# Stores of the paired-head tiles in 8 KB DMA packets, loads kept at 32 KB

## The chip, the cores and the metric

The kernel runs on one core of one Trainium2 chip, with the chip's other cores idle. The time is device time of one execution, in microseconds; executions of one kernel mostly agree within 0.3%. The core has 16 DMA engines, which move all loads and stores. In the profile's lines PE is the matrix engine (TensorE) and PEld its weight loads, ACT is ScalarE, DVE VectorE, POOL GpSimd and SP SyncE; a q after a name (SPq) is that engine's instruction queue. A transfer has landed when all 16 DMA engines have reported their part of it done, through a counter called a semaphore.

## The reference

It is the forward and backward pass of attention with one query per head. `k` and `v` (2 x 32 heads x 8192 x 128, bfloat16) are read, and gradients `dk`, `dv` of the same size are written, so 268 MB come in and 268 MB go out.

```python
scores = jnp.einsum("bhqd,bhkd->bhqk", q, k) * scale      # Sq = 1
p = softmax(scores)
out = jnp.einsum("bhqk,bhkd->bhqd", p, v)
_out, vjp = jax.vjp(fwd, q, k, v)
return (out, *vjp(grad_out))                              # out, dq, dk, dv
```

## The kernel before

Two heads form a pair; the pair's K (or V) is one tile of 128 partitions x 32 KB. Six such tiles are in SBUF, the core's on-chip memory. A tile is loaded, transposed and multiplied, then overwritten in place by its gradient and stored; only when that store has landed may the next load use the buffer. Loads are issued from SyncE (SP), stores from GpSimd (POOL). Whole tiles move in one DMA; each partition's 32 KB is one contiguous run in memory, so one tile is 128 packets of 32 KB, eight for each DMA engine.

```python
load_eng = nc.sync
store_eng = nc.gpsimd

def load(i, w, pieces=(NCH,)):                 # w: 0 is K, 1 is V
    t = kvp.tile([P, NT, D], BF16, tag=f"kv{slot_of(i, w)}", name="kvt")
    ...
    pin(load_eng.dma_start(out=t[:, n0:n1, :], in_=src[:, n0:n1, :]))

def outer(i, w, c, ends):                      # dk or dv in place of k or v
    pin(nc.vector.tensor_tensor(out=h.tile[w][:, n0 : n0 + CH, :]..., op=ALU.mult))
    if c + 1 in ends:
        ...
        pin(store_eng.dma_start(out=dst[:, b0:b1, :], in_=h.tile[w][:, b0:b1, :]))

# ... cut ...
whole = [NCH]
last_v = [NCH // 2, NCH]                       # the last pair is stored in parts
last_k = [NCH // 2, NCH - 2, NCH - 1, NCH]
for g in range(...):                           # 16 steps per pair, three pairs in flight
    if (i := at(O1 + NCH)) is not None and i + 3 < NP: load(i + 3, 0)
    if (i := at(O0 + NCH)) is not None and i + 3 < NP: load(i + 3, 1)
    if x := within(O1): outer(x[0], 1, x[1], last_v if x[0] == NP - 1 else whole)
    if x := within(O0): outer(x[0], 0, x[1], last_k if x[0] == NP - 1 else whole)
    ...                                        # transposes, scores, softmax, sums
```

Of the kernel before, what the change touches and what calls it, by code (L numbers as in the profile page):

```python
# [17 lines left out]
NG = 2  # L18
GH = 2
NTILE = 6  # L20


@with_exitstack
def kernel(
# [28 lines left out]
    store_eng = nc.gpsimd  # L53
    pin = tc.keep_in_program_order
# [25 lines left out]
    def slot_of(i, w):  # L80

        n = 2 * i + w
        return n if n < NTILE else slot_of(i - NTILE // 2, 1 - w)

    def load(i, w, pieces=(NCH,)):
        h = pairs_[i]
        t = kvp.tile([P, NT, D], BF16, tag=f"kv{slot_of(i, w)}", name="kvt")
        h.tile[w] = t
        src = (v_v if w else k_v)[i]
        c = 0  # L90
        for m in pieces:
            n0, n1 = c * CH, (c + m) * CH
            pin(load_eng.dma_start(out=t[:, n0:n1, :], in_=src[:, n0:n1, :]))  # L93
            c += m
# [7 lines left out]
    load(0, 1)  # L102
    for j in range(1, min(NTILE // 2, NP)):
        load(j, 0)
# [18 lines left out]
    for g in groups:  # L123
# [3 lines left out]
            out=par[g : g + CW], in_=rows.rearrange("p b h -> p h b"), axis=AX.X  # L127
# [298 lines left out]
    def outer(i, w, c, ends):  # L426

        h = pairs_[i]
        n0 = c * CH
        shape = [P, CH, D // 2, 2]  # L430
        pin(
            nc.vector.tensor_tensor(  # L432
                out=h.tile[w][:, n0 : n0 + CH, :].rearrange("p n (e t) -> p n e t", t=2),
                in0=h.qb[w][:]
                .rearrange("p (e t) -> p e t", t=2)
                .unsqueeze(1)
                .to_broadcast(shape),
                in1=h.pair[w][:, n0 : n0 + CH, :].unsqueeze(2).to_broadcast(shape),
                op=ALU.mult,
            )  # L440
        )
        if c + 1 in ends:
            at = ends.index(c + 1)
            b0, b1 = (ends[at - 1] if at else 0) * CH, (c + 1) * CH
            dst = (dv_v if w else dk_v)[i]
            pin(store_eng.dma_start(out=dst[:, b0:b1, :], in_=h.tile[w][:, b0:b1, :]))  # L446

    A1 = NCH + 4
    O1 = A1 + 1
# [7 lines left out]
    for g in range(SL * NP + O0 + NCH + 4 - SL):  # L457
# [15 lines left out]
        if x := within(O1):  # L473
            outer(x[0], 1, x[1], last_v if x[0] == NP - 1 else whole)
        if x := within(O0):
            outer(x[0], 0, x[1], last_k if x[0] == NP - 1 else whole)
# [77 lines left out]
```

## Time and profile before

The median was 1309.53 us of 3 runs (1307.43 to 1312.01).

| what | before |
|---|---|
| DMA queues' share of 16 engines' span | loads 49.5%, stores 48.2% |
| busy: PE / ACT / DVE | 88% / 75% / 65% |
| rate over the span, loads and stores alone | 410 GB/s |
| issue to landing, whole tile | load 27.8 us, store 40.2 us |

These are lines of the page of the kernel before: busy time of each engine, DMA busy tenths in 40 slices, and the DMA queues (packets, MB, share of the 16 engines' span).

```profile
PE 1147.5 (88%) x19108; PEld 849.1 (65%) x19108; DVE 850.5 (65%) x1551; ACT 984.3 (75%) x641; POOL 37.4 (3%) x76
...
DMA  9999999999999999999999999999999999999968
...
DMA packets 19933, 539.58 MB, mean 412 GB/s; under 512 B 2480, under 2 KB 2480, under 8 KB 2992
...
q1 hardware_dynamic: 9968, 268.51, 49.5%
q0 software_dynamic: 9792, 268.44, 48.2%
```

The two DMA queues add up to nearly 98%, and only the last two of 40 slices are not at 9: the DMA engines are the bound. PE comes next, but it mostly has work because data are there.

The page's lines of DMA issues (count, KB each, median us from issue to landing), and the line of the GpSimd issues among the groups (busy us, mean ns of one, idle time before):

```profile
out_dram<-kvt POOLq DMA_DIRECT2D x62, 4096.0 KB, 40.2
kvt<-in_v_dram SPq DMA_DIRECT2D x32, 4096.0 KB, 27.8
kvt<-in_k_dram SPq DMA_DIRECT2D x31, 4096.0 KB, 27.9
```

```profile
L446 POOL DMA_DIRECT2D out_dram<-kvt x68 | 36.3, 534 | 1261.7 <-DVE kvt L432 632.9
```

Who waits, from the waits of the SP queue and of all engines (us in total, times, longest):

```profile
SPq L93 <- DMA out_dram<-kvt: 1188.3, 58, 59.9
```

```profile
PE tp L183 <- DMA kvt<-in_k_dram: 76.8, 27, 5.0
...
PE tp L183 <- DMA kvt<-in_v_dram: 50.5, 27, 3.5
```

SP waits 1188 us for stores to land, because a landed store frees the buffer of a load. PE loses 127 us to loads, in pieces of a few us.

The table of stretches (from:to, length, busy us of each engine, then PE's clock, DMA share, GB/s):

```profile
100.00:200.00 100.00, 97.08 (x1713) 72.49 (x1711) 76.64 (x141) 88.02 (x59) 3.19 (x6) 0.98 1.01 430
200.00:400.00 200.00, 178.63 (x2968) 132.21 (x2965) 131.99 (x239) 152.75 (x100) 5.32 (x10) 0.92 1.00 427
400.00:600.00 200.00, 177.03 (x2940) 130.58 (x2938) 130.11 (x238) 150.97 (x100) 5.32 (x10) 0.92 1.00 419
600.00:800.00 200.00, 178.48 (x2933) 131.79 (x2929) 129.54 (x236) 150.99 (x99) 4.78 (x9) 0.91 1.00 413
1250.00:1265.00 15.00, 12.01 (x191) 8.77 (x189) 8.45 (x15) 9.88 (x6) 0.53 (x1) 0.89 0.76 323
1265.00:1270.00 5.00, 5.00 (x85) 3.75 (x85) 2.69 (x5) 4.17 (x4) 0.00 (x0) 0.99 0.17 72
1270.00:1275.00 5.00, 5.00 (x92) 3.61 (x89) 4.51 (x11) 4.84 (x6) 0.53 (x1) 1.00 0.03 10
```

The rate is 430 GB/s early and 413 to 419 after 400 us. Near the end there is a hole: at 1265-1275 us the DMA engines are nearly idle (shares 0.17 and 0.03). The chain of work that ended last, by engine:

```profile
issue 78%; DMA 14%; PE 3%; POOL 2%; DVE 1%; SPq 0%; POOLq 0%; ACT 0%; DVEq 0%; ACTq 0%
```

Below the page lie the packet records (queue, start, duration, size of every DMA packet). Several figures in this document are worked out from them. The undisturbed duration of a packet, called its minimum here, is 1213 ns for 32 KB, 611 for 16 KB, 309 for 8 KB, 159 for 4 KB: most packets take exactly that, and a few take 2 or 3 ns less. "Excess" below is the sum of what packets take above their minimum, divided by 16 engines.

### The profile page before, as it was taken

The page shows a single profiled execution, that of the slowest core. Times are in us where ns is not written, and L with a number is a line of the kernel's source. Part 1 is how long each engine was busy: PE and PEld are TensorE (multiplying, and loading weights), DVE is VectorE, ACT ScalarE, POOL GpSimd, SP SyncE. Part 2 cuts the span into 40 slices and gives each one's busy share as a digit, 9 for nine tenths or more (in the row PEclk, how much of TensorE's full clock was granted, in tenths as well). Part 3 has the DMA queues.
Part 4 walks back from the last instruction along what each step waited for, and adds up shares of the span by engine and source line. Part 5 has one row for each costly group of instructions (what it writes and reads, how often), then busy time and mean ns, then how long its engine had stood idle before and what let it go on. Part 6 is the DMA issues. An engine that isn't in the chain of part 4 may idle for free.

```text
span 1310.5 us, 41375 instructions
## 1 busy us (share of the span) xinstructions
PE 1147.5 (88%) x19108; PEld 849.1 (65%) x19108; DVE 850.5 (65%) x1551; ACT 984.3 (75%) x641; POOL 37.4 (3%) x76
## 2 busy tenths in 40 slices
PE   5999998898988988989889898898998988888894
PEld 4777766676766666666666676666666666666661
DVE  0677875766766767657676675665766757566666
ACT  5999987876877877778777787777876878777770
POOL 0000000000000000000000000000000000000000
PEclk9999998998989989889898898988988989888896
DMA  9999999999999999999999999999999999999968
GB/s 399 429 374 429 427 429 427 429 428 428 427 424 417 429 422 421 413 415 418 414 413 412 411 417 420 413 417 419 403 421 411 421 408 414 425 404 423 414 257 348
DMA packets 19933, 539.58 MB, mean 412 GB/s; under 512 B 2480, under 2 KB 2480, under 8 KB 2992
## 3 DMA queue, kind: packets, MB, share of 16 engines
q1 hardware_dynamic: 9968, 268.51, 49.5%
q0 software_dynamic: 9792, 268.44, 48.2%
q8 instruction: 149, 2.44, 0.7%
q14 instruction: 24, 0.20, 0.0%
HBM read 268.47 MB, written 268.47 MB: 410 GB/s over the span
## 4 chain that ended last, share of the span: by engine, by line
issue 78%; DMA 14%; PE 3%; POOL 2%; DVE 1%; SPq 0%; POOLq 0%; ACT 0%; DVEq 0%; ACTq 0%
DMA kvt<-in_v_dram 11%; DMA out_dram<-kvt 3%; POOL out_dram L446 2%; PE tp L183 1%; DVE kvt L432 1%; PE acc L376 1%; PE dpw L194 1%; POOLq L446 0%; PE sw L194 0%; ACT ev L185 0%; DVE sel L399 0%; SPq L93 0%; SPq L100 0%; PE sw L222 0%; PE acc L413 0%
## 5 line engine op out<-in xcount | busy, mean ns | idle before, releaser
L185 ACT COPY ev<-tp 128x2048 bf16<-128x2048 bf16 x512 | 954.0, 1865 | 293.6 <-PE tp L183 276.1
L183 PE MATMUL tp<-ident_bf,kvt 128*128 128x128 bf16 x8192 | 585.3, 229 | 127.3 <-DMA kvt<-in_k_dram 76.8
L432 DVE TENSOR_TENSOR kvt<-qb,pair 128x2048 bf16<-128x2048 bf16 x512 | 615.3, 1219 | 49.6 <-PE acc L376 46.7
L183 PEld LDWEIGHTS <-kvt 128*128 128x128 bf16 x8192 | 505.1, 103 | 137.2 <-DMA kvt<-in_k_dram 79.1
L194 PEld LDWEIGHTS <-ev 128*128 128x128 bf16 x8192 | 239.9, 96 | 218.0 <-issue 135.4
L376 PE MATMUL acc<-kvt,E_pad 128*64 128x512 bf16 x1024 | 173.1, 421 | 0.0
L376 PE MATMUL acc<-kvt,dS_pad 128*64 128x512 bf16 x1024 | 169.4, 416 | 1.0 <-DVE dS_pad L362 1.0
L194 PE MATMUL sw<-qdT,ev 128*128 128x2 bf16 x4096 | 142.0, 164 | 2.2 <-ACT ev L185 2.2
L194 PE MATMUL dpw<-qdT,ev 128*128 128x2 bf16 x4096 | 142.2, 164 | 1.0 <-ACT ev L185 1.0
L270 DVE CUSTOM_DVE_ANT_0 junk<-E_f,dpw 64x128 bf16<-64x128 f32 x64 | 18.3, 285 | 144.1 <-PE dpw L194 143.7
L207 DVE TENSOR_REDUCE mp<-sw 64x1 f32<-64x128 f32 x64 | 18.5, 289 | 108.5 <-PE sw L194 108.1
L446 POOL DMA_DIRECT2D out_dram<-kvt x68 | 36.3, 534 | 1261.7 <-DVE kvt L432 632.9
L399 DVE SCALAR_TENSOR_TENSOR sel<-acc,diag,sel 128x128 f32<-128x128 f32 x192 | 67.3, 351 | 6.8
L376 PEld LDWEIGHTS <-dS_pad 128*64 128x64 bf16 x1024 | 38.2, 112 | 29.4 <-issue 6.3
L376 PEld LDWEIGHTS <-E_pad 128*64 128x64 bf16 x1024 | 37.7, 112 | 26.8 <-issue 6.5
L262 DVE CAST E_pad<-E_f 64x128 bf16<-64x128 f32 x64 | 15.3, 239 | 48.5 <-ACT E_f L252 48.5
L413 PE MATMUL acc<-par,sel 128*128 128x2 f32 x128 | 22.0, 241 | 8.0 <-DVE sel L399 8.0
L176 DVE CAST qb<-dpw 128x128 bf16<-128x128 f32 x64 | 18.2, 284 | 13.4 <-PE dpw L167 13.4
L413 PEld LDWEIGHTS acc<-par,sel 128*128 128x128 f32 x128 | 19.7, 195 | 9.5 <-DVE sel L399 9.5
L340 DVE TENSOR_SCALAR negdelta<-dpw,rl 128x1 f32<-128x1 f32 x32 | 7.0, 218 | 27.0 <-PE dpw L300 27.0
L252 ACT ACTIVATE E_f<-sw,negm 64x128 f32<-64x128 f32 x64 | 23.2, 362 | 1.6
L352 DVE SCALAR_TENSOR_TENSOR dSu<-dpw,negdelta,E_f 64x128 f32<-64x128 f32 x64 | 22.4, 350 | 2.1
(49 smaller groups left out, 230.1 us busy)
## 6 DMA issues: line engine op xcount, KB each, us to landing
out_dram<-kvt POOLq DMA_DIRECT2D x62, 4096.0 KB, 40.2
kvt<-in_v_dram SPq DMA_DIRECT2D x32, 4096.0 KB, 27.8
kvt<-in_k_dram SPq DMA_DIRECT2D x31, 4096.0 KB, 27.9
out_dram<-kvt POOLq DMA_DIRECT2D x3, 2048.0 KB, 8.7
kvt<-in_k_dram SPq DMA_DIRECT2D x1, 2048.0 KB, 11.5
kvt<-in_k_dram SPq DMA_DIRECT2D x2, 512.0 KB, 4.5
kvt<-in_k_dram SPq DMA_DIRECT2D x1, 1024.0 KB, 6.9
out_dram<-kvt POOLq DMA_DIRECT2D x1, 1024.0 KB, 7.6
```

Of the source, the lines that this page charges most:

```text
L183: pin(nc.tensor.transpose(tp[:, t, :], src[:, c * CH + t, :], ident_bf[:]))
L185: pin(nc.scalar.copy(out=ev[:], in_=tp[:]))
L194: nc.tensor.matmul(dst[:, c * CH + t, :], lhsT=ev[:, t, :], rhs=qdT[:, w, GH * i : GH * (i + 1)], start=True, stop=True,)
L207: pin(nc.vector.reduce_max(out=h.mp[hs], in_=h.s[hs, :, g], axis=AX.X))
L252: nc.scalar.activation(out=h.E_f[hs], in_=h.s[hs, :, g], func=ACT.Exp, bias=h.negm[hs], scale=scale, accum_out=h.ld[hs, g : g + 1],)
L270: nc.vector.tensor_tensor_reduce(out=junk[hs], in0=h.E_f[hs], in1=h.dp[hs, :, g], scale=1.0, scalar=0.0, op0=ALU.mult, op1=ALU.add, accum_ ...
L352: nc.vector.scalar_tensor_tensor(out=dSu[hs], in0=h.dp[hs, :, g], scalar=negdelta[hs], in1=h.E_f[hs], op0=ALU.add, op1=ALU.mult,)
L376: nc.tensor.matmul(h.acc[w][g : g + CW, :], lhsT=wts[:, n0 * GH : n0 * GH + CW], rhs=rows[:, n0 : n0 + QT, :].rearrange("p n d -> p (n d)" ...
L399: nc.vector.scalar_tensor_tensor(out=h.sel[:], in0=block, scalar=diag[:, b : b + 1], in1=h.sel[:], op0=ALU.mult, op1=ALU.add,)
L413: nc.tensor.matmul(h.acc[w][:, 0:GH], lhsT=h.sel[:], rhs=par[:], start=True, stop=True)
L432: nc.vector.tensor_tensor(out=h.tile[w][:, n0 : n0 + CH, :].rearrange("p n (e t) -> p n e t", t=2), in0=h.qb[w][:] .rearrange("p (e t) -> ...
L446: pin(store_eng.dma_start(out=dst[:, b0:b1, :], in_=h.tile[w][:, b0:b1, :]))
```

## The change

The intent: an engine alternates between its load and store queue packet by packet. If a store packet is a quarter of a load packet, loads get four fifths of the bytes while both have work. Loads then land earlier, and compute waits less.

```diff
+RUN_S = 8192
...
-            pin(store_eng.dma_start(out=dst[:, b0:b1, :], in_=h.tile[w][:, b0:b1, :]))
+            pin(
+                store_eng.dma_start(
+                    out=dst[:, b0:b1, :], in_=h.tile[w][:, b0:b1, :], max_dma_last_dim=RUN_S
+                )
+            )
```

No instruction moves. The 62 whole-tile stores get four descriptors per partition, three half tiles get two, the last small ones stay as they were.

## The prediction

> **What bounds it now.** The DMA engines: the page gives the load queue 49.5% and the store queue 48.2% of 16 engines' span, and the slices show DMA at 9 in all but the last two. PE is busy 88%, ACT 75%. In the waits, PE loses only 127 us to loads, in pieces of 3 to 5 us, while SP spends 1188 us waiting for a store to land before it may refill a buffer. The table of stretches moves 430 GB/s at 100-200 us, 427 at 200-400, but 413 to 419 from 400 to 1000 us.
>
> The trace's packet records say why. An undisturbed 32 KB packet takes 1213 ns (8 KB 309): about 8 ns plus 0.0368 ns per byte. On an engine load and store packets alternate, as the Trainium skill says ("DMA: Bandwidth & Descriptors", Queues, rings and completion order: round-robin at packet granularity). Store packets average 1230 ns, load packets 1264: some 25 us per engine over the minimum, nearly all after 400 us. Those slow loads (1.4 to 2.3 us each) come in bursts where the store queue has run dry and loads run alone just after a store; from 100 to 400 us, with a backlog of stores, there are next to none.
>
> **What the change does.** No instruction moves; 65 of 68 stores get 4 or 2 descriptors per partition. Store-queue packets go from 9,792 to about 33,984.
> - Cost: 4 x 309 against 1213 ns, 23 ns per 32 KB, 496 per engine: +11.4 us of engine time, all on the bound resource (an estimate from those packets).
> - Shift: alternation is by packet, so while both queues have work loads get four fifths of the bytes, not half. A load should land 14-17 us after issue instead of 27.8; a store in 45-50 instead of 40.2. In a saturated ring of six tiles this alone gains nothing.
> - Gain 1: stores queue up behind loads, the store queue seldom runs dry, and part of the slow-load bursts goes: 0 to -20 us; I take -11.
> - Gain 2: around 1250-1275 us the engines idle for about 12.6 us (DMA shares 0.76, 0.17, 0.03 in those stretches), since the last load lands late and later stores wait for compute. With loads first, a backlog of stores fills that hole: -5 to -10; I take -7.
> - Possible loss: four times the software-made descriptors on GpSimd. An issue now takes 0.53 us and the first packet came 3.2 us later; backlog hides growth unless it nears the 20 us cadence.
>
> Sum: 1309.5 + 11.4 - 11 - 7 = 1303 us.
>
> **What would show it.** Right: 8 KB store packets at 309-315 ns; load issue-to-landing nearly halved, store landing longer; PE's waits on loads down; mean load packet at 1220-1240 ns; the hole before the last stores gone, so that the chain of waits ends on stores.
> Wrong: loads still average 1264 or more (then 1310-1315); the hole remains; or GpSimd issues lengthen to microseconds.
>
> **What would make it wrong.** One engine already runs its store packets at about 1300 ns; if that excess is per descriptor, not per byte, it would quadruple there and cost over 5%. The tail's 16 and 8 KB stores show no such growth, so I give it a small chance. In the other direction, if slow loads vanish and the hole closes, about 1285 us.
>
> Predicted 1303 us, range 1283 to 1328. Faster by over 2%: 0.14; within 2%: 0.75; slower by over 2%: 0.11.

## The result

With the change the median is 1307.99 us (1306.05 to 1309.61, 4 runs), before 1309.26 us. The ratio is 0.9988, 95% interval 0.9965 to 1.001. A ratio here is the mean time of one kernel's fast runs over that of the other's in the same rounds, so it is not quite the ratio of the medians. A later repeat gave 0.9999 (0.9986 to 1.0012). The time did not move, to within 0.2%.

The same lines of the page, with the change:

```profile
PE 1136.5 (87%) x19108; PEld 844.3 (65%) x19108; DVE 850.3 (65%) x1551; ACT 984.7 (75%) x641; POOL 51.1 (4%) x76
...
DMA  9999999999999999999999999999999999999987
...
DMA packets 44126, 539.58 MB, mean 413 GB/s; under 512 B 2481, under 2 KB 2481, under 8 KB 2993
...
q0 software_dynamic: 33984, 268.44, 49.7%
q1 hardware_dynamic: 9968, 268.51, 48.8%
```

```profile
out_dram<-kvt POOLq DMA_DIRECT2D x62, 4096.0 KB, 49.7
kvt<-in_v_dram SPq DMA_DIRECT2D x32, 4096.0 KB, 18.9
kvt<-in_k_dram SPq DMA_DIRECT2D x31, 4096.0 KB, 18.6
```

```profile
L448 POOL DMA_DIRECT2D out_dram<-kvt x68 | 50.0, 736 | 1240.0 <-DVE sel L394 637.2
```

Loads land in 18.6 to 18.9 us instead of 27.8, and stores in 49.7 instead of 40.2: the order at the engines did change as intended. The load queue's share fell from 49.5% to 48.8%, but the store queue's rose from 48.2% to 49.7%. A GpSimd issue takes 0.74 us instead of 0.53.

```profile
SPq L94 <- DMA out_dram<-kvt: 1196.1, 58, 60.0
```

```profile
PE tp L184 <- DMA kvt<-in_v_dram: 91.7, 26, 6.1
...
PE tp L184 <- DMA kvt<-in_k_dram: 36.0, 22, 5.1
```

The waits did not shrink: PE lost 127 us to loads before and 91.7 + 36.0 = 128 us now, though each load is over 9 us faster. SP still waits 1196 us, since stores land later.

```profile
100.00:200.00 100.00, 98.42 (x1763) 73.81 (x1761) 78.05 (x143) 90.64 (x60) 4.47 (x6) 1.00 1.01 420
200.00:400.00 200.00, 175.49 (x2939) 130.28 (x2936) 131.95 (x238) 152.10 (x100) 7.44 (x10) 0.92 1.01 422
400.00:600.00 200.00, 176.60 (x2927) 131.06 (x2927) 129.50 (x236) 149.92 (x98) 7.44 (x10) 0.91 1.01 420
600.00:800.00 200.00, 179.18 (x2991) 132.65 (x2991) 132.94 (x242) 154.11 (x102) 7.45 (x10) 0.92 1.00 418
1250.00:1265.00 15.00, 12.49 (x197) 9.08 (x196) 7.32 (x15) 10.51 (x10) 0.00 (x0) 0.89 0.87 356
1265.00:1270.00 5.00, 5.00 (x102) 4.06 (x100) 4.89 (x9) 4.83 (x3) 0.74 (x1) 1.00 0.63 256
1270.00:1275.00 5.00, 4.34 (x63) 2.13 (x60) 3.90 (x8) 2.09 (x2) 0.71 (x1) 1.00 1.01 413
```

The early rate fell from 430 to 420 GB/s, the later one rose from 413-419 to 418-420. The hole in the tail is partly filled (shares 0.87, 0.63, 1.01 in place of 0.76, 0.17, 0.03).

```profile
issue 86%; DMA 7%; POOL 3%; DVE 1%; PE 1%; SPq 0%; POOLq 0%; ACT 0%; DVEq 0%; ACTq 0%
```

The DMA part of the chain is 7% now (by line 4% stores and 3% V loads), where it was 14% (11% V loads and 3% stores).

### Where the time went

The packet records allow an account, in us per engine. "Overlap" is time in which more packets are on record than there are engines: a packet starts 3 to 4 ns before its predecessor on the same engine ends. "Idle" is time with fewer than 16 packets in flight, after the first load packet. Each column comes from one profiled run, so differences of 1 to 2 us mean little. The profiled run of the kernel before (1312.01 us) was also the slowest of its four, that of the change (1308.33 us) an average one.

| | before | the change | difference |
|---|---|---|---|
| packets at their minimum duration | 1242.6 | 1254.2 | +11.6 |
| overlap | -4.0 | -8.8 | -4.8 |
| excess of load packets | 26.4 | 16.0 | -10.4 |
| excess of store packets | 9.1 | 16.0 | +6.9 |
| idle engines | 20.0 | 14.6 | -5.4 |
| sum of these rows' differences | | | -2.1 |
| span of the profiled run | 1310.5 | 1306.6 | -3.9 |
| median of all runs | 1309.26 | 1307.99 | -1.3 |

The rows repeat in other profiles. e9, the change once more, differs from before by +11.6, -4.4, -10.1, +6.4 and -4.9 us. e8, whose first 28 pairs run as before, has a load excess of 24.3 and a store excess of 7.5 us; e7, whose first 28 pairs run as in the change, has 16.8 and 15.7.

So the change made loads cheaper and the tail fuller as hoped. The smaller packets and a new excess on the stores took it back. The experiments ask whether this account holds: what a small packet really costs, whether the order of loads and stores is worth anything, where the excess comes from, and how much of it is tail.

### The profile page after: what moved, and what is told of

The parts are those of the page before. It is cut to its first block, busy times and chain, and to the rows that moved or that the text cites. A ratio compares the mean times of both kernels' runs of the same rounds, so it can differ in the third digit from the quotient of the medians.

```text
span 1306.6 us, 41375 instructions
## 1 busy us (share of the span) xinstructions
PE 1136.5 (87%) x19108; PEld 844.3 (65%) x19108; DVE 850.3 (65%) x1551; ACT 984.7 (75%) x641; POOL 51.1 (4%) x76
## 3 DMA queue, kind: packets, MB, share of 16 engines
q0 software_dynamic: 33984, 268.44, 49.7%
q1 hardware_dynamic: 9968, 268.51, 48.8%
## 4 chain that ended last, share of the span: by engine, by line
issue 86%; DMA 7%; POOL 3%; DVE 1%; PE 1%; SPq 0%; POOLq 0%; ACT 0%; DVEq 0%; ACTq 0%
DMA out_dram<-kvt 4%; POOL out_dram L448 3%; DMA kvt<-in_v_dram 3%; DVE kvt L433 1%; PE tp L184 1%; PE acc L377 0%; PE dpw L195 0%; POOLq L448 0%; ACT ev L186 0%; DVE sel L400 0%; SPq L94 0%; SPq L101 0%; PE acc L414 0%; DVE dSu L353 0%; DVE sel L394 0%
## 5 line engine op out<-in xcount | busy, mean ns | idle before, releaser
L184 PE MATMUL tp<-ident_bf,kvt 128*128 128x128 bf16 x8192 | 581.7, 228 | 127.7 <-DMA kvt<-in_v_dram 91.7
L377 PE MATMUL acc<-kvt,dS_pad 128*64 128x512 bf16 x1024 | 172.8, 423 | 1.5 <-DVE dS_pad L363 1.5
L377 PE MATMUL acc<-kvt,E_pad 128*64 128x512 bf16 x1024 | 163.2, 400 | 0.0
L448 POOL DMA_DIRECT2D out_dram<-kvt x68 | 50.0, 736 | 1240.0 <-DVE sel L394 637.2
L271 DVE CUSTOM_DVE_ANT_0 junk<-E_f,dpw 64x128 bf16<-64x128 f32 x64 | 18.2, 285 | 85.5 <-PE dpw L195 85.0
L414 PE MATMUL acc<-par,sel 128*128 128x2 f32 x128 | 22.0, 241 | 10.1 <-DVE sel L400 10.1
L414 PEld LDWEIGHTS acc<-par,sel 128*128 128x128 f32 x128 | 19.7, 195 | 10.9 <-DVE sel L400 10.9
L177 DVE CAST qb<-dpw 128x128 bf16<-128x128 f32 x64 | 18.1, 283 | 13.2 <-PE dpw L168 13.2
L215 DVE TENSOR_REDUCE gm<-sw 1x2 f32<-1x128 f32 x32 | 8.9, 279 | 25.5 <-PE sw L212 25.5
L253 ACT ACTIVATE E_f<-sw,negm 64x128 f32<-64x128 f32 x64 | 23.2, 363 | 1.6
## 6 DMA issues: line engine op xcount, KB each, us to landing
out_dram<-kvt POOLq DMA_DIRECT2D x62, 4096.0 KB, 49.7
kvt<-in_v_dram SPq DMA_DIRECT2D x32, 4096.0 KB, 18.9
kvt<-in_k_dram SPq DMA_DIRECT2D x31, 4096.0 KB, 18.6
kvt<-in_k_dram SPq DMA_DIRECT2D x1, 2048.0 KB, 11.6
```

The costliest lines, as they stand in the source:

```text
L184: pin(nc.tensor.transpose(tp[:, t, :], src[:, c * CH + t, :], ident_bf[:]))
L253: nc.scalar.activation(out=h.E_f[hs], in_=h.s[hs, :, g], func=ACT.Exp, bias=h.negm[hs], scale=scale, accum_out=h.ld[hs, g : g + 1],)
L271: nc.vector.tensor_tensor_reduce(out=junk[hs], in0=h.E_f[hs], in1=h.dp[hs, :, g], scale=1.0, scalar=0.0, op0=ALU.mult, op1=ALU.add, accum_ ...
L377: nc.tensor.matmul(h.acc[w][g : g + CW, :], lhsT=wts[:, n0 * GH : n0 * GH + CW], rhs=rows[:, n0 : n0 + QT, :].rearrange("p n d -> p (n d)" ...
L414: nc.tensor.matmul(h.acc[w][:, 0:GH], lhsT=h.sel[:], rhs=par[:], start=True, stop=True)
```

## The experiments

Theory at the start: small packets cost engine time, and the gain comes from loads going first. The rivals: packet size has no effect at all; or small packets as such, not the order, take the slow loads away. Twelve runs were made, all with correct results; e9 and e10 repeat earlier kernels.

| run | edit | median us | ratio to before (95%) | load / store landing, us |
|---|---|---|---|---|
| e1 | loads 8 KB, stores 8 KB | 1311.26 | 1.0034 (1.0018-1.0051) | 25 / 43.7 |
| e2 | loads 8 KB, stores 32 KB | 1332.57 | 1.0183 (1.015-1.0216) | 47 / 18.0 |
| e3 | stores 16 KB | 1298.32 | 0.9934 (0.9919-0.9949) | 21 / 46.3 |
| e4 | stores 4 KB | 1309.19 | 1.0023 (1.0003-1.0042) | 17.5 / 51.0 |
| e5 | stores 32 KB from ScalarE's queue | 1305.29 | 0.999 (0.9968-1.0012) | 25 / 42.8 |
| e6 | loads 16 KB, stores 16 KB | 1303.68 | 0.9969 (0.9954-0.9984) | 29 / 39.4 |
| e7 | stores 8 KB for pairs 0-27 only | 1308.15 | 1.0003 (0.9981-1.0026) | 19 / 49.2 |
| e8 | stores 8 KB for the last four pairs only | 1305.63 | 0.9985 (0.9966-1.0003) | 28 / 40.3 |
| e9 | the change again | 1308.71 | 0.9999 (0.9986-1.0012) | 19 / 50.1 |
| e10 | stores 16 KB again | 1298.20 | 0.9918 (0.9904-0.9932) | 21 / 47.1 |
| e11 | e10, K of pair 30 stored in halves | 1298.22 | 0.9919 (0.9905-0.9933) | |
| e12 | e11, 8 KB for the last four pairs | 1298.19 | 0.9919 (0.9906-0.9933) | |

The same account for the runs that matter most, in us per engine (packet records, one profile each):

| | before | change | e1 | e2 | e3 | e4 | e6 |
|---|---|---|---|---|---|---|---|
| minimum | 1242.6 | 1254.2 | 1265.8 | 1254.2 | 1247.1 | 1272.6 | 1251.6 |
| overlap | -4.0 | -8.8 | -13.3 | -9.4 | -6.5 | -17.2 | -8.3 |
| load excess | 26.4 | 16.0 | 5.1 | 18.4 | 10.5 | 19.0 | 22.2 |
| store excess | 9.1 | 16.0 | 19.2 | 13.9 | 16.1 | 12.9 | 6.2 |
| idle | 20.0 | 14.6 | 16.8 | 35.9 | 14.9 | 5.5 | 15.5 |

### e1: both kinds of packet at 8 KB

```diff
-            pin(load_eng.dma_start(out=t[:, n0:n1, :], in_=src[:, n0:n1, :]))
+            pin(load_eng.dma_start(out=t[:, n0:n1, :], in_=src[:, n0:n1, :], max_dma_last_dim=8192))
```
(on top of the change)

> Loads and stores both in 8 KB packets: the cost of small packets without any shift in favour of loads (alternation is again half and half by bytes). Theory (small packets cost engine time; the gain of the change comes from loads going first, which keeps the store queue from running dry and fills the hole in the tail): 23 ns more per 32 KB on both queues, 11.4 + 11.6 us, plus some 7 us of store excess, slow loads and hole in the tail as in the kernel before: 1330 to 1342 us. Rival 1 (packet size costs nothing, nothing was gained either): 1305 to 1312. Rival 2 (small packets in themselves, not the order of loads and stores, took the slow loads away): 1312 to 1322, with the load excess per 32 KB well under the 51 ns of before.

It took 1311.26 us: 0.34% more than before, and nowhere near 1330. The forecast missed twice. The doubled packet count costs less than the sum of minimum durations says: that sum rises by 23.2 us, but 9.3 us of it is overlap. The time itself lies in the range of rival 1, but the other 13.9 us speak against it. And load excess fell to 5.1 us without any preference for loads, which speaks for rival 2. But it did not simply vanish: store excess rose to 19.2. The prediction's reading of the slow loads, that they come from a store queue that has run dry, was not enough.

### e2: the change turned round

```diff
-            pin(load_eng.dma_start(out=t[:, n0:n1, :], in_=src[:, n0:n1, :]))
+            pin(load_eng.dma_start(out=t[:, n0:n1, :], in_=src[:, n0:n1, :], max_dma_last_dim=8192))
```
(on top of the kernel before)

> The change turned round: loads in 8 KB packets, stores in 32 KB, so stores get four fifths while both queues have work. Theory: +11.6 us for load packets; stores land in under 30 us and loads take 40 or more; the store queue is dry more often and loads run alone more, so load excess per 32 KB is at least the 51 ns of before; the last load lands as late or later and the hole in the tail stays or grows: 1322 to 1345 us. Rival (order of loads and stores is worth nothing, slow loads have another cause): 1315 to 1321, load excess and hole unchanged.

1332.57 us, as the theory had it. e2 and the change add almost the same number of packets (24,321 and 24,193), and differ in which side is favoured: 1.8% slower against nothing. So the order of loads and stores is worth something, and the rival that denies it is out. The issue lines (count, KB each, median us to landing) show the preference reversed:

```profile
out_dram<-kvt POOLq DMA_DIRECT2D x62, 4096.0 KB, 18.0
kvt<-in_v_dram SPq DMA_DIRECT2D x32, 4096.0 KB, 46.6
```

The cost appears at the end, in e2's stretches after the last load was issued at 1230 us:

```profile
1270.00:1275.00 5.00, 0.00 (x0) 0.00 (x0) 0.00 (x0) 0.00 (x0) 0.00 (x0) 0.68 0.15 66
1275.00:1280.00 5.00, 0.00 (x0) 0.00 (x0) 0.00 (x0) 0.00 (x0) 0.00 (x0) 0.50 0.04 18
1280.00:1285.00 5.00, 4.90 (x52) 3.86 (x52) 1.42 (x3) 1.87 (x1) 0.00 (x0) 0.50 0.01 3
1285.00:1290.00 5.00, 5.00 (x82) 3.45 (x79) 2.23 (x6) 4.33 (x5) 0.00 (x0) 0.96 0.00 0
```

From 1270 to 1280 us PE does nothing (0.00), while the DMA share is 0.15 and 0.04: the last load hangs on one engine, and the others have nothing left. The 16 completion records of that load say it too: the median engine was done 19.3 us after issue, the last but one after 26.7, the last after 49.9. Load excess per 32 KB fell instead of rising, which was a miss.

### e3: stores at 16 KB

```diff
-RUN_S = 8192
+RUN_S = 16384
```

> Stores in 16 KB packets: two descriptors per partition, loads get two thirds. Theory: cost 2 x 611 - 1213 = 9 ns per 32 KB, 4.5 us, plus 2 to 4 us of excess; half or more of the gain on slow loads (mean load packet 1245 to 1255 ns) and of the hole in the tail: 1299 to 1307 us. Rival (size has no effect): 1305 to 1312 with load mean at 1264.

1298.32 us, ratio 0.9934: a real gain, just under the range forecast. The mean load packet took 1232 ns, also under the range given. A store's landing is between that of before and that of the change:

```profile
out_dram<-kvt POOLq DMA_DIRECT2D x62, 4096.0 KB, 46.3
kvt<-in_v_dram SPq DMA_DIRECT2D x32, 4096.0 KB, 21.2
```

The account shows why 16 KB beats 8 KB: minimum less overlap rises by only 2.0 us (4.5 - 2.5) against 6.8 with 8 KB, and load excess falls further, to 10.5. From the change to e3 the rows add up to -9.9 us; the spans differ by 10.0.

### e4: stores at 4 KB

```diff
-RUN_S = 8192
+RUN_S = 4096
```

> Stores in 4 KB packets: eight descriptors per partition, loads get eight ninths. Theory: cost 8 x 159 - 1213 = 59 ns per 32 KB, 29 us, plus 7 to 15 us of excess; gains hardly larger than with 8 KB (load mean 1235 to 1245 ns, hole gone): 1325 to 1340 us; GpSimd issue near 1.0 us. Rival (size has no effect): 1305 to 1312.

1309.19 us: slower by only 0.23%, so this forecast was far too high; the time lies in the rival's range. The minimum rises by 30.0 us, but overlap takes back 13.2, and idle time falls from 20.0 to 5.5. By this account size does matter, but gain and cost cancel at 4 KB as at 8 KB. The GpSimd issue took 0.86 us.

### e5: who writes the descriptors

The completion records of all transfers between 150 and 1240 us show that in the kernel before, a store's median engine (the ninth of the 16 to finish, here and below) is done 24.0 us after issue and its last engine after 40.4; a load's after 23.0 and 27.9. One engine lags, and the semaphore waits for it. Among the 7,936 store packets of 32 KB, 408 took 4 to 16% above minimum (mean 1318 ns), and in 98% of the sampled instants no more than one such packet was in flight. One engine's share of stores is 496 packets, so that fits one slow engine. Following an engine from packet to packet supports it (each packet joined to the only one that ended 1 to 8 ns after its start): after a store packet of this slow kind, the next store packet was slow too in 69% of cases, against 4% of all. In the records it can't be told which number it has.

```diff
-    store_eng = nc.gpsimd
+    store_eng = nc.scalar
```
(on top of the kernel before)

> Stores in 32 KB packets as before, but issued from ScalarE's queue, where the descriptors are not written by software on GpSimd. New theory after the first four runs: in the kernel before one of the 16 engines lags (a store's last engine lands 16 us after the median engine, a load's 4 to 10 us, the last load's 15 us), and every load and store counts as landed only with that engine; its store packets take about 1300 ns. If that comes from software descriptors, here the last engine lands within 2 to 4 us of the median, store packets all near 1213 to 1230 ns, and the time is 1280 to 1300 us. Rival (the laggard has to do with the engine or its memory, not with who writes descriptors): lag and 1300 ns packets remain, 1303 to 1315 us (ScalarE also waits for VectorE at each store, at most some us in all).

1305.29 us, ratio 0.999: no clear difference, in the rival's range. (The profiled run was the slowest of its six, 1312.62 us.) The stores are in the other kind of queue now, and still land after 42.8 us:

```profile
q10 hardware_dynamic: 9792, 268.44, 48.9%
...
out_dram<-kvt ACTq DMA_DIRECT2D x62, 4096.0 KB, 42.8
kvt<-in_v_dram SPq DMA_DIRECT2D x32, 4096.0 KB, 25.6
```

499 store packets were slow in the same manner (mean 1309 ns). The laggard does not come from descriptors written in software on GpSimd; the theory was wrong there. Its cause stays open. The change itself answers another fear of the prediction. Were the laggard's 105 ns (1318 - 1213) due per descriptor, it would have over 1,600 packets of 8 KB near 414 ns (408 x 4); the change has about 150 between 389 and 509 ns, and 1,211 that are 4 to 16% over their minimum (mean 333 ns). So the handicap goes by bytes, not by descriptors.

### e6: both at 16 KB

```diff
-RUN_S = 8192
+RUN_S = 16384
...
-            pin(load_eng.dma_start(out=t[:, n0:n1, :], in_=src[:, n0:n1, :]))
+            pin(load_eng.dma_start(out=t[:, n0:n1, :], in_=src[:, n0:n1, :], max_dma_last_dim=RUN_S))
```

> Loads and stores both in 16 KB packets, to be set against stores alone at 16 KB (1298 us): same packets for stores, but no shift in favour of loads. A packet starts 3 to 4 ns before its predecessor ends, so the real cost is 2 x (611 - 3.5) - (1213 - 3.5), 5.5 ns per 32 KB, near 3 us on each queue. Theory that loads going first is worth 5 to 10 us at equal store size (it takes the laggard out of the loads' landing): 1302 to 1310 us, last load landing 5 us or more behind its median engine. Rival (only the packets' size counts): 1296 to 1301.

1303.68 us, within the theory's range. Against e3 (0.9934) and its repeat (0.9918), the same stores with loads of equal packets give 0.9969: 0.3 to 0.5% less gain, 5 to 7 us. Not all of that is the preference. The loads' own smaller packets cost 2.7 us in the account (minimum less overlap, e6 against e3), so the preference itself is worth perhaps 2 to 4 us, which no run isolates. And e6 is 0.3% faster than the kernel before with no preference at all. The last load's last engine landed 28.9 us after issue, its median engine after 21.6; in e3 20.7 and 18.9. So the preference takes the laggard out of the loads' landing. Over the loads between 150 and 1240 us the last engine comes this much after the median: before 4.9 us, the change 2.0, e1 3.2, e2 18.2, e3 2.0, e4 1.6, e6 6.0.

### e7 and e8: the bulk and the tail apart

```diff
-                    out=dst[:, b0:b1, :], in_=h.tile[w][:, b0:b1, :], max_dma_last_dim=RUN_S
+                    ..., max_dma_last_dim=32768 if i >= NP - 4 else RUN_S      # e7
+                    ..., max_dma_last_dim=RUN_S if i >= NP - 4 else 32768      # e8
```

> 8 KB store packets for pairs 0 to 27 and 32 KB for the last four: pays the cost of the change in full, without its gain in the tail. Theory (the gain is the last load's earlier landing and the filled hole in the tail, the bulk runs at best even): 1309 to 1316 us, the last load's last engine 8 us or more behind the median. Rival (the gain is spread over the whole run): within 2 us of the change itself, 1305 to 1309.

> 32 KB store packets for pairs 0 to 27 and 8 KB for the last four: an eighth of the cost, all of the gain in the tail. Theory: 1299 to 1305 us, last load's last engine within 5 us of the median, hole in the tail smaller. Rival (gain spread over the whole run): 1305 to 1310.

e7 took 1308.15 us (ratio 1.0003), e8 1305.63 us (0.9985). Neither is clear of no effect, and both times lie in the rivals' ranges, just outside the theories'. In the bulk, cost and gain cancel. In the tail alone, at an eighth of the cost, the gain was about 2 us, if any, less than forecast, although the last load landed 13 us earlier than before (1245 in place of 1258 us, last load packet). An earlier last load does not make an equally earlier end: the stores that it overtook are still to be done. For e7 the forecast of 8 us between median and last engine can't be judged: of its last load eight engines were done by 18.1 us after issue and the other eight from 25.8 to 29.9.

### e9 to e12: repeats, and attempts to go further

e9 is the change, e10 is e3, both unaltered. e11 adds one more cut, e12 another:

```diff
-            outer(x[0], 0, x[1], last_k if x[0] == NP - 1 else whole)
+            outer(x[0], 0, x[1], last_k if x[0] == NP - 1 else last_v if x[0] == NP - 2 else whole)   # e11, e12
...
-                    ..., max_dma_last_dim=RUN_S
+                    ..., max_dma_last_dim=8192 if i >= NP - 4 else RUN_S                                # e12
```

> The change itself once more, so that it stands beside the 16 KB version on one chip: 1305 to 1309 us, ratio 0.997 to 1.001; store-packet mean 315 to 318 ns, load mean 1240 to 1248 ns as before.

> Stores in 16 KB packets once more. If its gain is real: ratio 0.991 to 0.995, 1296 to 1300 us, clear of the change itself on the same chip. If the first result was luck of one chip: 1302 or more.

> 16 KB store packets, and the K tile of the last pair but one stored in two halves, so that its first half is there about 8 us earlier for the hole in the tail (DMA shares 0.57 and 0.46 at 1250-1260 us with 16 KB alone, near 5 us idle). Theory: the end of that run is held up by stores queued after the hole, so 2 to 4 us less than 16 KB alone, 1294 to 1297 us. Rival (the end waits on compute): no difference.

> As the run before, with 8 KB store packets for the last four pairs, so that the last loads go still further ahead. Theory: last load's issue to landing 17 to 19 us instead of 20 to 22, and 0 to 4 us less than the run before: 1291 to 1297 us. Rival (later stores give back what earlier loads win): no difference.

On one chip the change is at 0.9999 and 16 KB at 0.9918, 10.5 us apart by medians; both repeat. e11 and e12 add nothing, so the rivals' "no difference" was right; which of the two reasons they name holds is not shown. In e12 the last load landed in 19.1 us where e11's took 21.3, and the end did not move. Filling the hole in the tail is not in itself a gain. From the last load's landing to the last store's issue there are about 38 us in the kernel before and in e10 to e12 (before 1261.1 to 1299.1; e12 1242.7 to 1280.7), and 11 to 15 us of final stores follow; where the loads come earlier, more stores are left for the end.

### Where the excess sits

For this the excess was sorted by the time since each load's and each store's issue (sums over the transfers of a run, us per engine, from one profile each).

| run | excess close to a start | of all of its kind |
|---|---|---|
| before | loads 19.7, within 6 us of a store's issue | 26.4 |
| e2 | loads 10.9, 1 to 5 us after a store's issue | 18.4 |
| the change | stores 7.7, 3 to 5 us after a load's issue | 16.0 |
| e1 | stores 12.1, 3 to 5 us after a load's issue | 19.2 |
| e3 | stores 6.8, 3 to 5 us after a load's issue | 16.1 |

An even spread over the 20 us between transfers would put 7.9 us of the first row into 6 us, and 1.6 us of the third into 2 us. (In e9, the repeat of the change, the third row is 4.6 of 15.5; in e10 the last is 6.2 of 16.1.) So many of the slow packets are those in flight while the other queue starts on a new transfer. In the change and e3 no load bytes at all move in the three us before a load's first packets, so the load queue has run dry, and the store packets in flight at its restart are the stretched ones. In e2, 80 to 85% of the bytes are loads just before a store's first packets, and it is the loads that are stretched. In the kernel before, a load's and a store's issue lie close together and on average half the bytes are stores, so the first row alone would not tell which start matters. In the change and in e4 a second burst, of load excess, comes 13 to 16 us after a load's issue, near its end (about 6 and 12 us); e3 and e10 have none, which is much of why 16 KB has the lower load excess. That the restart is the cause is read from these times alone, and why a packet would be stretched then is not shown by any of these runs.

## Why the prediction was right or wrong

- The bound, right: the DMA engines, before and after.
- The shift, right in kind: store landing was forecast at 45 to 50 us and measured at 49.7; loads at 14 to 17 us, measured 18.6 to 18.9. That "in a saturated ring of six tiles this alone gains nothing" was not tested by itself; e6 against e3 points to 2 to 4 us. The V loads' share of the chain fell from 11% to 3%, and the stores' is 4%.
- The cost, over-sized. "4 x 309 against 1213 ns, 23 ns per 32 KB ... +11.4 us". A packet starts 3 to 4 ns before the one in front of it ends, so the real spacing is about 306 and 1209.5 ns, 14 to 15 ns per 32 KB, near 7 us. The account gives 11.6 - 4.8 = 6.8.
- Gain 1, the step that failed: "the store queue seldom runs dry, and part of the slow-load bursts goes ... I take -11". Two things in it were wrong. First, the store queue did not run dry less often. Take the loads between 100 and 1240 us whose predecessor on their engine the records give (about 80%, joined as in e5): it was another load in 9% of cases before, in 9% with the change and in 23% in e9. Before, slow loads (over 16% above the minimum) did come after another load, in 53% of cases; with the change in 8%, in e9 in 19%. So load excess fell by 10.4 us, near the -11 taken, but not for the reason given: that agreement is luck, and why it fell stays open. Second, the step left out the stores. With the change it is the load queue that runs dry and restarts for each tile, and store excess rose by 6.9 us (mean 316.8 ns, over the 309 to 315 given). In this profile 6.4 of the 6.9 lie 3 to 5 us after a load's issue, when its first packets come (7.7 against 1.3 before); in e9 it is 3.3 of 6.4. The net of this term is -3.5, not -11.
- Gain 2, a little over-sized as a count of idle time: -7 forecast, -5.4 measured, with 3.6 of that after the last load. e8, e11 and e12 then show that less idle time in the tail is not the same as an earlier end.
- PE's waits on loads were to go down and did not (127 and 128 us). The mean load packet was 1243 ns, just over the 1220 to 1240 named.
- The feared loss by descriptors on GpSimd did not come: 0.74 us per issue, and the slow engine's excess goes by bytes.

The sum was 11.4 - 11 - 7 = -6.6; the measured terms are 6.8 - 3.5 - 5.4 = -2.1, and the medians say -1.3 us, with a repeat at a ratio of 0.9999. The measured time lies within the forecast range, but the small gain that was named is not there.

The remedy that the runs found is stores at 16 KB: 1298.2 us, 0.7 and 0.8% better than the kernel before in two runs on two chips, and 0.8% better than the change on the chip that ran both.

## What to carry to other kernels

When two DMA queues alternate packet by packet, the ratio of packet sizes sets who goes first; favour the side whose landing the rest waits for, and try the mildest ratio first, since here two to one gained 0.7 to 0.8% and four to one nothing. Try equal smaller packets beside it: both sides at 16 KB gained 0.3%. On a DMA-bound kernel, count what a change does to every queue, because time saved on loads may turn up on stores. Look at the landing of a transfer's last engine as well as at the median engine, as a single slow engine decides when a semaphore fires.

## What the Trainium skill lacked or had wrong

- "DMA: Bandwidth & Descriptors", Queues, rings and completion order, says that engines take turns between queues at packet granularity. The trace agrees that they take turns: loads and stores alternate one for one at 32 KB (91% of loads follow a store), and with the change 32 KB load packets alternate with 8 KB store packets. The page counts 9 to 17 descriptors to a typical packet; here the turn passes after one record, and there is one record per descriptor (7,936 for 62 stores of 128 partitions). What the page lacks is the use of it: packet size as a priority (load landing 27.8 us, 18.6 to 18.9 with 8 KB stores, 47 with 8 KB loads).
- The same page, Why small descriptors are slow (HBM only), gives a fixed overhead of about 3 cycles per packet. The trace has spacings of about 155.5, 306 and 1209.5 ns for 4, 8 and 32 KB, which leave near 5 ns per packet. With the 32-byte beats of the same passage, the other 1204.6 ns of a 32 KB packet are 1,024 beats of 1.18 ns, so three cycles would be 3.5 ns (an estimate): of that order, but less than measured. The page doesn't say that recorded packet durations overlap by 3 to 4 ns, so that their sum overstates the cost by about 13 us at 68,000 packets (e1).
- The same page, Latency and other measured facts, takes slow engines 7 and 15 to be specific to software descriptors, as a guess that it calls uncertain. One engine lagged here too (its number isn't in the trace), and it lagged in the same manner with stores from ScalarE's queue (e5: 499 slow packets against 408), so this does not support the guess.
- The same page, Issuing engines are not separate DMA queues, says that all issuers share the same 16 engines; e5 agrees (0.999), so nothing is lacking there.
- "Perfetto Trace Analysis", DMA Instruction — SWDGE (GPSIMD), says that the profiled time of a GpSimd DMA ends with descriptor generation. The page gives no figure for it: here 0.53 us for one descriptor per partition, 0.74 for four, 0.86 for eight (means over all issues).
- No page has the packets that are stretched while the other queue starts on a transfer (19.7 us of load excess within 6 us of a store's issue in the kernel before), nor their cause.
